# Decode attention with an MLP: group loads in a loop, wq and the last group inside TensorE's loop, heads transposed on VectorE, and a branch hint

## The chip, the core and the metric

The kernel runs on one core of a Trainium2 chip. A core has five engines, each with its own program: TensorE (PE, matmuls), VectorE (DVE), ScalarE (ACT), GpSimd (POOL) and SyncE (SP), which here only issues transfers. They meet in semaphores. Data moves from memory into the on-chip buffer by 16 DMA engines; matmuls write to PSUM. The metric is the device time of one execution in microseconds.

## The reference, cut to what matters

```python
xn = layernorm(x)                                    # x: 4 x 1 x 512
q  = (xn @ wq) as 4 x 32 heads x 128                 # wq: 512 x 4096
p  = softmax(q . k_cache * 128**-0.5)                # k_cache: 4 x 32 x 4096 x 128
o  = p . v_cache                                     # v_cache: the same shape
A   = o as 4 x 4096 @ wo                              # wo: 4096 x 512
B   = x1 + gelu(layernorm(x1) @ w3) @ w4              # w3: 512 x 1792, w4: 1792 x 512
out = x + A + B
```

x1 is xn: with one position the spatial shift leaves only zeros, so w1 and w2 have no effect and are not read. All is float32. K and V are 268 MB each; with wq, wo, w3 and w4 561 MB are read once.

## The kernel before

The 128 heads of the 4 batches are worked off in `NG` = 32 groups of 4 heads. One group's K, and one group's V, is a tile of 128 partitions x 16,384 columns (8.39 MB): partitions 32t to 32t+31 hold head t, each a stretch of 64 KB. Three such slots exist: K alternates between S1 (even groups) and S0 (odd groups), V lies in S2.

What is done for one group: VectorE spreads the query over the partitions (`qx`, `qb`, lines 324 and 327), multiplies K by it in place, in two halves (lines 330 and 332), sums over the 128 columns of each row (335, into `sc`), and finds the maximum (337 to 340). ScalarE takes the exponentials into `pw` (238). TensorE multiplies `pw` with V in 32 matmuls of 512 columns into `pv` (167); one small matmul sums the denominators (171); ScalarE copies `pv` (244); four small matmuls pick the heads out (176); and ScalarE keeps the result in `OS` (246). Then V's slot is free.

SP's program is written out, one instruction for each transfer. It issues V(g), waits until the sum over K(g) is done (`k_free`), issues K(g+2), waits until V(g) is used (`v_free`), and so on (lines 133 to 139). All its transfers stand in one queue in that order. At the start it issues wq in two halves into S2 and the first K in two halves; K(1) and V(0) wait for the query (`d_T`, line 131). The second half of the first K is passed on by POOL (lines 159, 160). At the end the last V goes to S1 as soon as K(30) is used up (141), w3 and w4 go to S2 when V(30) is used (143, 144), and wo goes to S0 in six pieces when K(31) is used (148).

TensorE's program is the query's matmuls (190), a loop over 31 groups, then, written out: three "spreads" of the heads of a batch over the partitions by a matmul (181), the last group's V, w3 (207), the last spread, and w4 (217). In a second block of code (from line 365) it multiplies wo piece by piece: rows 0 to 23 of each partition into `y`, in 512 columns, the others straight into `total`, in four quarters; ScalarE copies `y`, and four matmuls add that copy to `total` (381). Two copies and two transfers write the output.

Between the two blocks all engines meet.

Of the kernel before, what the change touches and what calls it, by code (L numbers as in the profile page):

```python
# [7 lines left out]
F32 = mybir.dt.float32  # L8
# [5 lines left out]
P = 128  # L14
# [6 lines left out]
def decode_block(ctx: ExitStack, tc: tile.TileContext, x, k, v, wq, wo, w3, w4, out):  # L21
# [26 lines left out]
    X = sbuf("X", [P, WC, B])  # L48
# [3 lines left out]
    mask = sbuf("mask", [P, 4])  # L52
# [7 lines left out]
    ot = sbuf("ot", [P, JB, HG])  # L60
    rec = sbuf("rec", [P, JB, HG])
    lt = sbuf("lt", [P, H, 4])

    pv, oz, total, y, pa, pb = (nc.alloc_psum_tensor(f"ps{i}", [P, 512], F32) for i in range(6))
# [7 lines left out]
    PIECES = ((0, 8), (8, 16), (16, 24), (24, 28), (28, 31), (31, 32))  # L72
    CUT = 24
    s_x, s_v, s_vl, s_kh, s_h = (sem(n) for n in ("sx", "sv", "svl", "skh", "sh"))
    s_wq = [sem(f"swq{n}") for n in range(2)]
    s_k = [sem(f"sk{n}") for n in range(2)]
    s_wo = s_k + [s_v, s_x, s_kh, s_h]
    d_self, g_a, c_done, d_T, k_free, v_free = (sem(n) for n in ("dself", "ga", "cd", "dT", "kf", "vf"))
# [6 lines left out]
    def group(flat, g):  # L85
        n = HG * S * DH
        return flat[g * n:(g + 1) * n].rearrange("(p r) -> p r", p=P)
# [4 lines left out]
    q_sb = S0[:, 4 * D:6 * D].rearrange("p (n f) -> p n f", n=2)  # L92
    qT = S0[:, 6 * D:8 * D]
    xp = S0[:, 8 * D:8 * D + 2 * P].rearrange("p (e c i) -> p e c i", e=2, c=NC)
    xnT = S0[:, 9 * D:9 * D + P].rearrange("p (c m) -> p c m", c=NC)
    wq_sb = S2[:, :].rearrange("p (c n) -> p c n", c=NC)
    w3_sb = S2[:, :NC * F].rearrange("p (c f) -> p c f", c=NC)
    w34 = NC * F + NF * D
    w4_sb = S2[:, NC * F:w34].rearrange("p (m n) -> p m n", m=NF)
    hs, gu, gt, gT = (S2[:, w34 + n * FT:w34 + (n + 1) * FT] for n in range(4))  # L100
    V3 = S2[:, :].rearrange("p (c d) -> p c d", c=C)
    VL = S1[:, :].rearrange("p (c d) -> p c d", c=C)
# [10 lines left out]

    with tc.tile_critical(no_gpsimd_drain=True), nc.Block(no_gpsimd_drain=True) as block:

        @block.sync
        def _(e):
            def load_k(g):
                e.dma_start(KS[g % 2][:, :], group(kf, g)).then_inc(s_k[g % 2], 16)

            def load_k_half(g, n, s):
                r = slice(n * ROW // 2, (n + 1) * ROW // 2)
                e.dma_start(KS[g % 2][:, r], group(kf, g)[:, r]).then_inc(s, 16)

            wq_r = wq.rearrange("(p c) n -> p c n", p=P)
            for n in range(2):
                c = slice(n * NC // 2, (n + 1) * NC // 2)
                e.dma_start(wq_sb[:, c, :], wq_r[:, c, :]).then_inc(s_wq[n], 16)
            load_k_half(0, 0, s_k[0])
            load_k_half(0, 1, s_kh)  # L130
            e.wait_ge(d_T, 2)
            load_k(1)
            for g in range(NG - 1):
                if g > 0:
                    take(e, v_free)
                e.dma_start(S2[:, :], group(vf, g)).then_inc(s_v, 16)
                if g + 2 < NG:
                    take(e, k_free)
                    load_k(g + 2)
            take(e, k_free)  # L140
            e.dma_start(S1[:, :], group(vf, NG - 1)).then_inc(s_vl, 16)
            take(e, v_free)
            e.dma_start(w3_sb, w3.rearrange("(p c) f -> p c f", p=P)).then_inc(s_wq[0], 16)
            e.dma_start(w4_sb, w4.rearrange("(p m) n -> p m n", p=P)).then_inc(s_wq[1], 16)
            take(e, k_free)
            wo_r = wo.rearrange("(p c) n -> p c n", p=P)
            for n, (c0, c1) in enumerate(PIECES):
                e.dma_start(wo_sb[:, c0:c1, :], wo_r[:, c0:c1, :]).then_inc(s_wo[n], 16)  # L148

        @block.gpsimd  # L150
        def _(e):
            e.memset(xs, 0.0).then_inc(g_a, 1)
            e.memset(ident[:, :], 0.0).then_inc(c_done, 1)
            e.memset(rs[:, :], 0.0)
            e.memset(pw[:, :, :], 0.0).then_inc(g_a, 1)
# [3 lines left out]
            take(e, s_kh, 16)  # L159
            e.wait_ge(c_done, 2).then_inc(s_h, NG)  # L160

        @block.tensor
        def _(e):
            def contract(V):
                for g in range(G4):
                    t = g % 4
                    i = mm(e, pv[32 * t:32 * t + 32, :], pw[:, g, :], V[:, 4 * g:4 * g + 4, :], g < 4, g >= G4 - 4)
                return i

            def outputs(done):  # L170
                i = mm(e, oz[:, HG:2 * HG], ones[:, :], rs[:, :], True, True)
                if done is not None:
                    i.then_inc(done, 1)
# [4 lines left out]

            def spread(b):
                take(e, d_p)  # L180
                mm(e, pa[:, 32 * b:32 * b + 32], lt[:, :, :], sel[:, :], True, True).then_inc(p_a, 1)

            e.wait_ge(d_T, 1)
            for c in range(NC):
                if c % (NC // 2) == 0:
                    take(e, s_wq[c // (NC // 2)], 16)
                w = wq_sb[:, c, :].rearrange("p (n j h d) -> p n h j d", n=2, j=JB // 2, h=HG)
                for n in range(2):
                    for h in range(HG):
                        i = mm(e, (pa, pb)[n][32 * h:32 * h + 32, :], xnT[:, c, :], w[:, n, h], c == 0, c == NC - 1)  # L190
                    if c == NC - 1:
                        i.then_inc(p_a, 1)

            with nc.Fori(0, NG - 1, 1, engines=[ET.PE]):
                take(e, s_v, 16)
                take(e, a_p)
                contract(V3).then_inc(p_a, 1)
                outputs(v_free)
            for b in range(B - 1):
                spread(b)  # L200
            take(e, a_p)
            take(e, s_vl, 16)
            contract(VL).then_inc(p_a, 1)
            e.wait_ge(s_wq[0], 16)
            for c in range(NC):
                for t in range(4):
                    i = mm(e, pb[32 * t:32 * t + 32, :FT], x1T[:, c, :], w3_sb[:, c, t * FT:(t + 1) * FT],
                           c == 0, c == NC - 1)
            i.then_inc(p_a, 1)
            outputs(None)  # L210
            spread(B - 1)
            mm(e, total[:, 0:P], ident[:, :], base[:, :], True, False)
            e.wait_ge(s_wq[1], 16)
            e.wait_ge(d_p, 1)
# [5 lines left out]
        def _(e):  # L220
# [5 lines left out]
            for n in range(2):  # L226
                take(e, p_a)
                e.mul(q_sb[:, n, :], (pa, pb)[n][:, :], DH ** -0.5).then_inc(a_d, 1)
            e.wait_ge(d_T, 2)
            e.activation(os[:, 0, 0:1], st[:, 3:4], AF.Exp)  # L230
            take(e, g_a)

            def weights():
# [6 lines left out]
                i.then_inc(a_p, 1)  # L240

            def outputs(o):
                take(e, p_a)
                e.copy(os[:, :, :], pv[:, :].rearrange("p (m d) -> p m d", m=4)).then_inc(a_p, 1)  # L244
# [3 lines left out]
            def spread(b):  # L248
                take(e, p_a)
                return e.copy(X[:, :, b], pa[:, 32 * b:32 * b + 32])  # L250

            with nc.Fori(0, NG - 1, 1, engines=[ET.Activation]) as g:
                weights()
                e.drain().then_inc(a_d, 1)
                outputs(OS[:, bass.ds(g, 1), :])
            weights()
            e.drain().then_inc(a_d, 1)
            for b in range(B - 1):
                spread(b).then_inc(c_done, 1)
            take(e, p_a)  # L260
            e.copy(os[:, :, :], pv[:, :].rearrange("p (m d) -> p m d", m=4)).then_inc(a_p, 1)
            take(e, p_a)
            e.copy(hs.rearrange("p (m i) -> p m i", i=32),
                   pb[:, :FT].rearrange("p (i m) -> p m i", i=32)).then_inc(a_d, 1)
            take(e, p_a)
            e.copy(OS[:, NG - 1:NG, :], oz[:, 0:2 * HG].unsqueeze(1)).then_inc(a_d, 1)
            e.wait_ge(d_a, 1)
            e.activation(gt, gu, AF.Tanh, scale=GELU_A).then_inc(a_d, 1)
            spread(B - 1)

        @block.vector
        def _(e):
            def own(i, n=1):
                i.then_inc(d_self, 1)
                take(e, d_self, n)
# [5 lines left out]
            own(e.reduce_sum(mask[:, :], ident[:, :].rearrange("p (q m) -> p q m", q=4), axis=AX.X))  # L281
# [142 lines left out]
```

## Time and profile before

| what | value |
|---|---|
| three runs | 1304.78, 1305.07, 1305.14 us; median 1305.07 |
| profiled execution, own time | 1304.94 us |
| its span, first to last instruction | 1303.2 us |
| read from memory | 561.00 MB, 430 GB/s over the span |
| mean granted TensorE clock | 0.627 |

Most rows of a profile give a line of the program, an engine, an operation, then the tile written and the tiles read. In a row of groups there follow the shapes, the count, the busy time in us and the mean of one in ns, and last the engine's idle time ahead of the group with what ended it. In a row in order of time the start and the length in us stand first. `SPq` is SP's queue: its rows are the moments at which a transfer is issued, not the transfer itself, and the profile gives the landing apart. `PEld` is TensorE's load of weights; a float32 matmul shows as two records and two loads.

### The profile page before, as it was taken

What the parts mean: (1) busy time and instruction counts of PE and PEld (TensorE: products, weight loads), DVE (VectorE), ACT (ScalarE), POOL (GpSimd) and SP (SyncE); (2) the same over time, 40 slices, a digit from 0 to 9 for tenths busy, and PEclk for the clock granted to TensorE, in tenths of its full rate; (3) what the DMA queues carried; (4) which work ended last, traced back from release to release, by engine and by line L of the source; (5) the groups of instructions that cost most, each with busy time, mean ns of one, the idle gap of its engine ahead of it and who ended that gap; (6) DMA issues with size and microseconds to landing.
All of it is one profiled execution on the core that took longest, in us unless ns stands there. A gap on an engine that the chain in (4) does not pass through costs nothing. (4 is left out here: it accounts for less than half of the span.)

```text
span 1303.2 us, 7027 instructions
## 1 busy us (share of the span) xinstructions
PE 364.8 (28%) x2622; PEld 130.6 (10%) x2622; DVE 1169.3 (90%) x343; ACT 98.9 (8%) x335; POOL 2.1 (0%) x9
## 2 busy tenths in 40 slices
PE   2032123333113333213333212333311333321347
PEld 0010001111001111001111000111000111100112
DVE  4999999999999999999999999999999999999971
ACT  1000000000000000000000000000000000000010
POOL 0000000000000000000000000000000000000000
PEclk9565566666566666566666556666556666655669
DMA  9999999999999999999999999999999999999998
GB/s 403 435 447 422 447 420 449 420 447 422 430 437 424 445 422 447 422 447 422 447 420 449 421 447 422 439 428 428 441 422 447 422 445 424 445 424 445 422 429 347
DMA packets 10830, 561.08 MB, mean 431 GB/s; under 512 B 1212, under 2 KB 1220, under 8 KB 1480
## 3 DMA queue, kind: packets, MB, share of 16 engines
q1 hardware_dynamic: 10808, 561.00, 99.6%
q8 instruction: 3, 0.05, 0.0%
q14 instruction: 3, 0.02, 0.0%
q10 hardware_dynamic: 16, 0.01, 0.0%
HBM read 561.00 MB, written 0.01 MB: 430 GB/s over the span
## 5 line engine op out<-in xcount | busy, mean ns | idle before, releaser
L335 DVE TENSOR_REDUCE sc<-slot 128x128 f32<-128x16384 f32 x32 | 551.0, 17220 | 8.2 <-DVEq L70 8.2
L112 PE MATMUL ps<-slot,pw 128*32 128x512 f32 x2048 | 294.9, 740 | 882.2 <-PEq L70 882.2
L330 DVE TENSOR_TENSOR slot<-slot,qb 128x8192 f32<-128x8192 f32 x32 | 278.1, 8692 | 43.6 <-DVEq L70 43.6
L332 DVE TENSOR_TENSOR slot<-slot,qb 128x8192 f32<-128x8192 f32 x32 | 277.9, 8684 | 2.1 <-DVEq L70 2.1
L112 PEld LDWEIGHTS ps<-slot,pw 128*32 128x32 f32 x2048 | 80.7, 133 | 1071.0 <-issue 1070.9
L238 ACT ACTIVATE pw<-sc,st 32x128 f32<-32x128 f32 x128 | 67.3, 525 | 243.0 <-ACTq L70 241.5
L244 ACT COPY os<-ps 128x512 f32<-128x512 f32 x31 | 18.1, 585 | 857.1 <-ACTq L70 857.1
L112 PE MATMUL ps<-sel,os 128*128 128x4 f32 x256 | 32.8, 252 | 17.5 <-PEq L70 17.5
L112 PEld LDWEIGHTS ps<-sel,os 128*128 128x128 f32 x256 | 31.0, 191 | 19.3 <-issue 19.3
L238 ACT ACTIVATION_READ_ACCUMULATOR pw<-sc,st 32x1 f32 x128 | 26.1, 204 | 0.0
L112 PE MATMUL ps<-slot 128*32 128x512 f32 x92 | 14.0, 747 | 18.8 <-PEq L70 17.6
L327 DVE STREAM_TRANSPOSE qb<-qx 128x128 f32<-128x128 f32 x32 | 10.0, 311 | 4.9 <-DVEq L70 0.5
L386 DVE COPY res<-ps 64x128 f32<-64x128 f32 x1 | 0.3, 283 | 15.2 <-PE ps L112 15.2
L337 DVE TENSOR_REDUCE st<-sc 128x1 f32<-128x128 f32 x32 | 9.2, 286 | 4.7
L356 DVE TENSOR_TENSOR slot<-slot 128x448 f32<-128x448 f32 x1 | 0.6, 624 | 13.1 <-DVEq L70 13.1
L112 PE MATMUL ps<-rs,ones 128*128 128x4 f32 x64 | 12.3, 263 | 0.0
L112 PEld LDWEIGHTS ps<-rs,ones 128*128 128x128 f32 x64 | 9.5, 188 | 26.7 <-issue 26.7
L324 DVE COPY qx<-Q 128x128 f32 x32 | 7.3, 227 | 4.9 <-issue 4.6
L339 DVE STREAM_TRANSPOSE mt<-mx 128x32 f32<-128x32 f32 x32 | 6.8, 211 | 4.7
L340 DVE TENSOR_REDUCE st<-mt 128x1 f32<-128x32 f32 x32 | 6.0, 186 | 4.8 <-DVEq L70 1.8
L338 DVE COPY mx<-st 128x32 f32<-128x32 f32 x32 | 5.8, 181 | 4.7
L246 ACT COPY OS<-ps 128x8 f32 x31 | 5.1, 165 | 42.4 <-ACTq L70 42.4
(58 smaller groups left out, 54.2 us busy)
## 6 DMA issues: line engine op xcount, KB each, us to landing
slot<-in_A_wq_dram SPq DMA_DIRECT2D x2, 4096.0 KB, 16.8
slot<-in_A_k_cache_dram SPq DMA_DIRECT2D x2, 4096.0 KB, 35.8
slot<-in_B_w_dram SPq DMA_DIRECT2D x2, 3584.0 KB, 22.7
slot<-in_A_wo_dram SPq DMA_DIRECT2D x3, 2048.0 KB, 30.1
slot<-in_A_wo_dram SPq DMA_DIRECT2D x1, 1024.0 KB
slot<-in_A_wo_dram SPq DMA_DIRECT2D x1, 768.0 KB, 37.9
slot<-in_A_v_cache_dram SPq DMA_DIRECT2D x32, 28.8
slot<-in_A_k_cache_dram SPq DMA_DIRECT2D x31, 42.3
```

The source lines that it names most:

```text
L112: return e.matmul(o, l, r, start=start, stop=stop)
L238: i = e.activation(o, sc[r, :].rearrange("p (g w) -> p g w", w=4), AF.Exp, bias=st[r, 1:2], scale=1.0, accum_out=rs[r, h:h + 1])
L244: e.copy(os[:, :, :], pv[:, :].rearrange("p (m d) -> p m d", m=4)).then_inc(a_p, 1)
L324: own(e.tensor_copy(qx[:, :].rearrange("p (h r) -> p h r", h=4), Q[:, bass.ds(g + n, 1), :].rearrange("p o h -> p (o h)").unsqueeze(2) .to ...
L327: own(e.transpose(qb[:, :], qx[:, :]))
L330: e.tensor_tensor(out=K[:, :C // 2, :], in0=K[:, :C // 2, :], in1=qw, op=ALU.mult).then_inc(d_self, 1)
L332: e.tensor_tensor(out=K[:, C // 2:, :], in0=K[:, C // 2:, :], in1=qw, op=ALU.mult).then_inc(d_self, 1)
L335: e.reduce_sum(sc[:, :], K, axis=AX.X).then_inc(d_self, 1)
L337: own(e.reduce_max(st[:, 0:1], sc[:, :], axis=AX.X), 2)
L338: own(e.tensor_copy(mx[:, :], st[:, 0:1].to_broadcast([P, 32])))
L339: own(e.transpose(mt[:, :], mx[:, :]))
L340: e.tensor_reduce(st[:, 1:2], mt[:, :], axis=AX.X, op=ALU.max, negate=True).then_inc(d_a, 1)
```

## The change

- A group is now made of four heads that lie four apart (`n t e` in the views `kf` and `vf`), so the source of each load of K and V is 4 x 32 rows of 64 KB, the four stretches of 32 rows 8.4 MB apart, where it was 128 rows in one stretch. The tile on the chip is the same.
- SP issues the groups' loads in a loop of 8 turns with 4 groups each; the addresses come from registers. The first K is one load. wq is loaded as 20/32 and 12/32 of each row; so is the last V.
- At the end w3 and w4 come first, into S1, and the last V comes behind them, into S2.
- TensorE's loop has 33 turns: the first multiplies wq by the input, which VectorE has written into columns 16 to 23 of `pw`; the last is the last group, with w3's matmuls ahead of it behind a branch. In each turn the last 12 of the 32 matmuls wait for `v_rest`, which POOL passes on for the first and the last turn and gives in advance for the others.
- ScalarE scales no query any more and runs its loop over all 32 groups; in the last turn it does its part of the MLP behind a branch.
- VectorE multiplies K in one instruction. The heads are turned by a transpose of 32 x 32 blocks (24 groups, and later the last 8) in place of the spreads. With that wo is read with its rows in another order, as 4 x 32 rows.
- wo's pieces end at rows 12, 20, 25, 28, 31 and 32 (before: 8, 16, 24, 28, 31 and 32), and rows 0 to 27 go into `y`.
- VectorE's program is aligned, and TensorE's program begins with a hint for the branch behind its last matmul, with padding behind that branch.

The core of the diff, with "..." where lines are left out:

```diff
+    X = sbuf("X", [P, B, H])
...
-    PIECES = ((0, 8), (8, 16), (16, 24), (24, 28), (28, 31), (31, 32))
-    CUT = 24
+    PIECES = ((0, 12), (12, 20), (20, 25), (25, 28), (28, 31), (31, 32))
+    CUT = 28
+    GF = 20
...
-    kf = k.rearrange("b h s d -> (b h s d)")
-    vf = v.rearrange("b h s d -> (b h s d)")
+    NB = B * 2
+    kf = k.rearrange("b (n t e) s d -> (b n) e t (s d)", n=2, t=HG).rearrange("m e t (p r) -> m e t p r", p=32)
+    vf = v.rearrange("b (n t e) s d -> (b n) e t (s d)", n=2, t=HG).rearrange("m e t (p r) -> m e t p r", p=32)
...
+    nc.vector.addr_align(128, offset=100, max_nops=0)
+    ahead = nc.tensor.mark_branch_hint_location()
...
+            e.dma_start(S2[:, FIRST], wq_r[:, FIRST]).then_inc(s_v, 16)
+            e.dma_start(S2[:, REST], wq_r[:, REST]).then_inc(s_q, 16)
+            load_k(0, 0)
+            e.wait_ge(d_T, 1)
+            load_k(0, 1)
+            with nc.Fori(0, NB, 1, engines=[ET.SP]) as m:
+                for i in range(3):
+                    load_v(m, i)
                     take(e, k_free)
+                    if i < 2:
+                        load_k(m, i + 2)
+                e.br_lt(m, NB - 1, on_true="sp_more", on_false="sp_next")
+                with nc.body("sp_more", valid_engines=[ET.SP]):
...
+                    load_k(after, 0)
+                    load_v(m, 3)
+                    take(e, k_free)
+                    load_k(after, 1)
+                    nc.br("sp_next", engines=[ET.SP])
+                nc.switch_bb("sp_next")
+            e.dma_start(w3_sb, w3.rearrange("(p c) f -> p c f", p=P)).then_inc(s_w3, 16)
+            e.dma_start(w4_sb, w4.rearrange("(p m) n -> p m n", p=P)).then_inc(s_w4, 16)
+            take(e, v_free)
+            last = src(vf, NB - 1, 3)
+            e.dma_start(S2[:, FIRST], last[:, :, FIRST]).then_inc(s_v, 16)
+            e.dma_start(S2[:, REST], last[:, :, REST]).then_inc(s_q, 16)
             take(e, k_free)
...
+            wo_r = wo.rearrange("(h q c) n -> q h (c n)", h=H, q=4)
...
+            with nc.Fori(0, NG + 1, 1, engines=pe) as g:
+                e.br_lt(g, NG, on_true="pe_turn", on_false="pe_mlp")
...
+                take(e, s_v, 16)
+                take(e, a_p)
+                for n in range(G4):
+                    if n == GF:
+                        take(e, v_rest)
+                    t = n % 4
+                    i = mm(e, pv[32 * t:32 * t + 32, :], pw[:, n, :], V[:, 4 * n:4 * n + 4, :], n < 4, n >= G4 - 4)
...
-                    e.tensor_tensor(out=K[:, :C // 2, :], in0=K[:, :C // 2, :], in1=qw, op=ALU.mult).then_inc(d_self, 1)
-                    take(e, s_h)
-                    e.tensor_tensor(out=K[:, C // 2:, :], in0=K[:, C // 2:, :], in1=qw, op=ALU.mult).then_inc(d_self, 1)
+                    own(e.tensor_tensor(out=K, in0=K, in1=qb[:, :].unsqueeze(1).to_broadcast([P, C, DH]), op=ALU.mult))
...
+                return e.transpose(X[:, b0:b1, :].rearrange("p b h -> p (b h)"), ot[:, b0:b1, :].rearrange("p b h -> p (b h)"))
...
         i.then_inc(g_a, 1)
+        e.br("pe_last").branch_hint(ahead)
+        with nc.body("pe_gap", valid_engines=[ET.PE]):
+            e.addr_align(256, offset=16, max_nops=0)
+            nc.br("pe_last", engines=[ET.PE])
+        nc.switch_bb("pe_last")
```

How the order of the program moves is seen best on the two engines on which the end rests. First SP's queue at its end, before (a row: line, operation, destination and source, shape of the tile):

```order
L119 DMA slot<-in_A_k_cache_dram 128x16384
L136 DMA slot<-in_A_v_cache_dram 128x16384
L141 DMA slot<-in_A_v_cache_dram 128x16384
L143 DMA slot<-in_B_w_dram 128x7168
L144 DMA slot<-in_B_w_dram 128x7168
L148 DMA slot<-in_A_wo_dram 128x4096 x3
L148 DMA slot<-in_A_wo_dram 128x2048
L148 DMA slot<-in_A_wo_dram 128x1536
L148 DMA slot<-in_A_wo_dram 128x512
```

And with the change, from the loop's end on:

```order
L130 REGISTER_ALU
L130 COMPARE_AND_BRANCH
L146 DMA slot<-in_B_w_dram 128x7168
L147 DMA slot<-in_B_w_dram 128x7168
L150 DMA slot<-in_A_v_cache_dram 128x1x10240
L151 DMA slot<-in_A_v_cache_dram 128x1x6144
L155 DMA slot<-in_A_wo_dram 128x1x6144
L155 DMA slot<-in_A_wo_dram 128x1x4096
L155 DMA slot<-in_A_wo_dram 128x1x2560
L155 DMA slot<-in_A_wo_dram 128x1x1536 x2
L155 DMA slot<-in_A_wo_dram 128x1x512
```

The last V has moved behind w3 and w4 and stands in two parts directly ahead of wo. Now TensorE from behind its loop to wo, before (`lt` is a batch's heads for a spread, `x1T` the MLP's input, `X` the heads for wo):

```order
L112 MATMUL ps<-sel,lt 128x32 x3
L112 MATMUL ps<-slot,pw 32x512 x32
L112 MATMUL ps<-slot,x1T 32x448 x16
L112 MATMUL ps<-rs,ones 128x4
L112 MATMUL ps<-sel,os 128x4 x4
L112 MATMUL ps<-sel,lt 128x32
L112 MATMUL ps<-base,ident 128x128
L112 MATMUL ps<-slot 32x512 x14
L114 UNCONDITIONAL_BRANCH x2
L419 UNCONDITIONAL_BRANCH
L112 MATMUL ps<-slot,X 4x512 x24
```

And with the change, from the MLP's code in the loop (run in the last turn alone) to wo:

```order
L105 MATMUL ps<-slot,x1T 32x448 x16
L183 UNCONDITIONAL_BRANCH
L105 MATMUL ps<-slot,pw 32x512 x32
L105 MATMUL ps<-rs,ones 128x4
L105 MATMUL ps<-sel,os 128x4 x4
L174 REGISTER_ALU
L174 COMPARE_AND_BRANCH
L105 MATMUL ps<-base,ident 128x128
L105 MATMUL ps<-slot 32x512 x14
L109 UNCONDITIONAL_BRANCH x2
L414 UNCONDITIONAL_BRANCH
L105 MATMUL ps<-slot,X 4x512 x28
```

The spreads are gone, w3's matmuls have moved ahead of the last V's, and 28 matmuls of 512 columns with wo stand where 24 stood.

More of the change, by code (lines that the diff above doesn't have):

```diff
@@ L59, in decode_block @@
     res = sbuf("res", [2 * 32, 2, P])
[L60 to L64, printed above, removed]
+    ot = sbuf("ot", [P, B, H])
+    rec = sbuf("rec", [P, NG, HG])
+    warm = sbuf("warm", [P, 1])
+    pv, oz, total, y, pb = (nc.alloc_psum_tensor(f"ps{i}", [P, 512], F32) for i in range(5))
     def sem(name):
@@ L117, in _ @@
         def _(e):
[L118 to L128, printed above, removed]
@@ L142, in _, with src, load_k @@
[L142 to L146, printed above, removed]
+            def src(flat, m, i):
+                return flat[m, i] if isinstance(m, int) else flat[bass.ds(m, 1), i].rearrange("m t p r -> (m t) p r")
+            def load_k(m, i):
+                e.dma_start(KS[i % 2][:, :], src(kf, m, i)).then_inc(s_k[i % 2], 16)
@@ L154, in _ @@
             e.memset(rs[:, :], 0.0)
-            e.memset(pw[:, :, :], 0.0).then_inc(g_a, 1)
+            e.memset(pw[:, :, :], 0.0)
             e.wait_ge(c_done, 1)
@@ L177, in outputs @@
                 i.then_inc(p_a, 1)
[L179 to L211, printed above, removed]
             mm(e, total[:, 0:P], ident[:, :], base[:, :], True, False)
-            e.wait_ge(s_wq[1], 16)
-            e.wait_ge(d_p, 1)
+            e.wait_ge(s_w4, 16)
+            take(e, d_p)
             for m in range(NF):
@@ L225, in _, with values @@
                 e.activation(st[:, 2:3], st[:, 1:2], AF.Sqrt, bias=st[:, 3:4], scale=1.0 / D).then_inc(a_d, 1)
-            for n in range(2):
+            def values():
                 take(e, p_a)
[L228 to L231, printed above, removed]
+                return e.copy(os[:, :, :], pv[:, :].rearrange("p (m d) -> p m d", m=4)).then_inc(a_p, 1)
+            values()
+            e.drain().then_inc(a_d, 1)
+            take(e, p_a)
+            e.activation(warm[:, :], st[:, 3:4], AF.Exp)
             def weights():
@@ L240, in weights @@
                 i.then_inc(a_p, 1)
+                e.drain().then_inc(a_d, 1)
             def outputs(o):
-                take(e, p_a)
-                e.copy(os[:, :, :], pv[:, :].rearrange("p (m d) -> p m d", m=4)).then_inc(a_p, 1)
+                values()
                 take(e, p_a)
                 return e.copy(o, oz[:, 0:2 * HG].unsqueeze(1))
[L248 to L252, printed above, removed]
+            act = [ET.Activation]
@@ L253, in _ @@
+            with nc.Fori(0, NG, 1, engines=act) as g:
                 weights()
-                e.drain().then_inc(a_d, 1)
+                e.br_lt(g, NG - 1, on_true="act_values", on_false="act_mlp")
+                with nc.body("act_mlp", valid_engines=act):
+                    take(e, p_a)
+                    e.copy(hs.rearrange("p (m i) -> p m i", i=32),
+                           pb[:, :FT].rearrange("p (i m) -> p m i", i=32)).then_inc(a_d, 1)
+                    take(e, d_a)
+                    e.activation(gt, gu, AF.Tanh, scale=GELU_A).then_inc(a_d, 1)
+                    nc.br("act_values", engines=act)
+                nc.switch_bb("act_values")
@@ L255, in _ @@
                 outputs(OS[:, bass.ds(g, 1), :])
-            weights()
             e.drain().then_inc(a_d, 1)
[L258 to L269, printed above, removed]
         @block.vector
         def _(e):
-            def own(i, n=1):
+            done = [0]
+            def mark(i):
                 i.then_inc(d_self, 1)
-                take(e, d_self, n)
+                done[0] += 1
+            def own(i):
+                mark(i)
+                e.wait_ge(d_self, done[0])
@@ L277, in _, with clear, rows @@
+            def clear():
+                take(e, d_self, done[0])
+                done[0] = 0
+            def rows(t):
+                return slice(32 * t, 32 * t + 32)
             e.memset(ones[:, :], 1.0)
@@ L358, in _ @@
             e.tensor_mul(gu, gu, hs).then_inc(d_a, 1)
-            normalised(B - 1)
-            e.wait_ge(a_d, 1)
+            take(e, a_d)
             own(e.tensor_scalar(gt, gt, 1.0, 0.5, op0=ALU.add, op1=ALU.mult))
```

153 lines of the change are left out of this document (72 added, 81 removed).

## The prediction

> **What bounds the kernel now.** I read the page first, then the stretches of time, then the queue's issues in order of time, then the chain that ended last. From the page: the engines' busy time and two DMA queues (packets, MB, share of 16 engines' span).
>
> ```profile
> PE 364.8 (28%) x2622; PEld 130.6 (10%) x2622; DVE 1169.3 (90%) x343; ACT 98.9 (8%) x335; POOL 2.1 (0%) x9
> ...
> q1 hardware_dynamic: 10808, 561.00, 99.6%
> ...
> q10 hardware_dynamic: 16, 0.01, 0.0%
> ```
>
> VectorE looks like the bound at 90%, but SP's queue is at 99.6%. The stretches decide it (start:end, length, then each engine's busy time, the granted clock, the DMA share and GB/s):
>
> ```profile
> 0.00:3.00 3.00, 0.00 (x0) 0.00 (x0) 0.29 (x3) 0.00 (x0) 2.09 (x9) 1.00 0.60 175
> ...
> 100.00:400.00 300.00, 83.07 (x570) 29.20 (x574) 286.40 (x73) 22.16 (x78) 0.00 (x0) 0.60 1.00 433
> 400.00:700.00 300.00, 76.66 (x544) 28.01 (x536) 277.52 (x73) 22.86 (x80) 0.00 (x0) 0.61 1.00 433
> 700.00:1000.00 300.00, 85.01 (x592) 30.45 (x592) 277.78 (x71) 22.86 (x80) 0.00 (x0) 0.62 1.00 433
> ...
> 1290.00:1295.00 5.00, 3.94 (x40) 0.90 (x44) 0.00 (x0) 0.00 (x0) 0.00 (x0) 1.00 0.96 403
> 1295.00:1299.00 4.00, 2.81 (x60) 1.27 (x56) 0.00 (x0) 0.58 (x1) 0.00 (x0) 1.00 0.69 275
> ```
>
> Three stretches of 300 us give 433 GB/s at a DMA share of 1.00, although VectorE's work in them differs by 9 us. So the transfers set the pace. VectorE's groups and the landings say the same:
>
> ```profile
> L335 DVE TENSOR_REDUCE sc<-slot 128x128 f32<-128x16384 f32 x32 | 551.0, 17220 | 8.2 <-DVEq L70 8.2
> L330 DVE TENSOR_TENSOR slot<-slot,qb 128x8192 f32<-128x8192 f32 x32 | 278.1, 8692 | 43.6 <-DVEq L70 43.6
> L332 DVE TENSOR_TENSOR slot<-slot,qb 128x8192 f32<-128x8192 f32 x32 | 277.9, 8684 | 2.1 <-DVEq L70 2.1
> ```
> ```profile
> slot<-in_A_v_cache_dram SPq DMA_DIRECT2D x32, 28.8
> slot<-in_A_k_cache_dram SPq DMA_DIRECT2D x31, 42.3
> ```
>
> VectorE waits 43.6/32 = 1.4 us per group for K. A load of 8.39 MB takes 8.39/433 = 19.4 us by itself but lands 28.8 us after its issue (V) and 42.3 us (K): when a load is issued, 9.4 us and 22.9 us of earlier work still stand in the queue. That is the cover which the issuing side has. The queue's own issues (start, length, line):
>
> ```profile
> 29.18 0.33 SPq L119 DMA_DIRECT2D slot<-in_A_k_cache_dram  x1
> 29.55 0.43 SPq L136 DMA_DIRECT2D slot<-in_A_v_cache_dram  x1
> 69.84 0.33 SPq L119 DMA_DIRECT2D slot<-in_A_k_cache_dram  x1
> 91.67 0.33 SPq L136 DMA_DIRECT2D slot<-in_A_v_cache_dram  x1
> ...
> 407.68 0.33 SPq L119 DMA_DIRECT2D slot<-in_A_k_cache_dram  x1
> ...
> 1181.72 0.33 SPq L119 DMA_DIRECT2D slot<-in_A_k_cache_dram  x1
> 1214.54 0.33 SPq L136 DMA_DIRECT2D slot<-in_A_v_cache_dram  x1
> 1220.42 0.33 SPq L141 DMA_DIRECT2D slot<-in_A_v_cache_dram  x1
> 1252.67 0.33 SPq L143 DMA_DIRECT2D slot<-in_B_w_dram  x1
> ...
> 1259.13 2.70 SPq L148 DMA_DIRECT2D slot<-in_A_wo_dram  x6
> ```
>
> Twenty periods lie between 407.68 and 1181.72: 38.70 us each, and 16.78 MB per period is again 433 GB/s. The chain that ended last is the stream's end and little else:
>
> ```profile
> 1260.93 37.92 DMA slot<-in_A_wo_dram
> ...
> 1298.89 1.10 PE ps L112 x32
> ...
> 1300.02 0.28 DVE res L386
> ```
>
> So 561.0 MB at 433 GB/s is 1295.6 us; with about 1.8 us before the first byte (3 us x 175 is 0.53 MB, or 1.2 us of the stream) that ends near 1297.4; the stream ends at 1298.85, and 1303.2 - 1298.85 = 4.35 us follow. The execution's own time is 1304.94, 1.74 over its span; the median of the three runs is 1305.07, 0.13 above it. I sum against 1304.94.
>
> **The change part by part.** *Bytes:* the same 561.0 MB; wq, the last V and wo are only cut differently. At 433 GB/s: 0.
>
> *The loop's arithmetic.* Two multiplications (8.69 + 8.68) become one over 16,384 columns, about 17.4 us, and a semaphore step goes: under 0.2 us per group from an engine that already waits 1.4. Nothing at the end: 0. SP's loop adds register work before each issue; an issue takes 0.33 us, and if it tripled, 9.4 us of queue cover V and 22.9 cover K: 0. TensorE's jump over the MLP's code in each turn stands before the wait for V: 0; should it cost 1 us after V has landed, the 9.4 still hide it.
>
> *The start.* K's first load is no longer halved, so VectorE begins its first group later. The rows (V's landings: least, median, most):
>
> ```profile
> 43.51 8.69 DVE L332 TENSOR_TENSOR slot<-slot,qb 128x8192 f32<-128x8192 f32 x1 [2.13 <-DVEq L70]
> ```
> ```profile
> DMA to landing us min/median/max: 28.1/28.8/52.4
> ```
>
> The second half of K came at about 43.4. Now the whole multiplication starts there and ends at 60.8, and the reduction at about 78.3, against 69.84 now: VectorE is 8.5 us later. K2 is issued on that, and the queue then still holds V0, which landed at 29.55 + 52.4 = 81.95: 3.6 us are left, so the queue does not run dry. The next two: V1 waits for TensorE's turn after V0's landing, as now (91.67); K3 comes at about 78.3 + 37.3 = 115.6, five us before V1's landing at 81.95 + 2 x 19.4 = 120.7. VectorE then needs 38.70 - 1.4 = 37.3 us a group when it need not wait, and wins 1.4 back in each. Cost 0; if the queue should run dry at K2, up to 2 us (an issue's start-up, from the 1.8 us before the first byte, beyond what the 3.6 covers). K1 waits for Q: one transpose of 512 columns and one copy instead of 1024 columns and two scalings against two small copies and a memset ahead of the matmuls; within 1 us of 29.18, while K0 lands at 43.4: 14 us of cover, 0.
>
> *The tail* is where cover is thin. w3 and w4 now come before the last V. Issue times stay (1220.42, 1252.67, 1259.13), and at 1252.67 the queue still holds about half of w3 and w4 (7.34 MB, 17 us, behind V30, which had landed when TensorE began on it at 1243.71), so it is not empty. The last V now ends where wo begins, 19.4 us before 1298.85: at 1279.5, its first 20/32 at 1272.2. TensorE's new wait, for the rest of wq or of this V by way of POOL, holds back its last 12 matmuls and the sums behind them; POOL releases the turns between ahead of time. ScalarE's last turn now waits for the MLP's matmuls and VectorE's GELU before it copies sums: w3 lands near 1252, so this is over near 1266, long before 1283. From 1272.2 TensorE has a row of work. Its rows at two paces (two matmuls are four loads), the steps after a group's matmuls, and the present tail:
>
> ```profile
> 1285.79 0.23 PEld L112 LDWEIGHTS ps<-slot 128*32 128x32 f32 x4 [0.63 <-issue]
> 1286.64 0.22 PEld L112 LDWEIGHTS ps<-slot 128*32 128x32 f32 x4 [0.63 <-issue]
> ...
> 1292.34 0.11 PEld L112 LDWEIGHTS ps<-slot,X 128*4 128x4 f32 x4 [0.32 <-issue]
> 1292.77 0.11 PEld L112 LDWEIGHTS ps<-slot,X 128*4 128x4 f32 x4 [0.32 <-issue]
> ```
> ```profile
> 1214.06 0.39 PE L112 MATMUL ps<-rs,ones 128*128 128x4 f32 x2
> ...
> 1216.24 0.17 ACT L246 COPY OS<-ps 128x8 f32 x1 [1.37 <-ACTq L70]
> ...
> 1243.71 8.55 PE L112 MATMUL ps<-slot,pw 128*32 128x512 f32 x64 [27.67 <-PEq L70]
> ...
> 1284.96 4.96 PE L112 MATMUL ps<-slot 128*32 128x512 f32 x28 [1.19 <-DVE slot L363]
> ...
> 1291.06 5.37 PE L112 MATMUL ps<-slot,X 128*4 128x512 f32 x48 [1.13 <-SPq L365]
> ...
> 1296.50 0.58 ACT L384 COPY os<-ps 128x512 f32<-128x512 f32 x1 [12.69 <-PE ps L112]
> ```
>
> A 512-column matmul takes 0.43 us after an idle stretch and 0.21 once running. The last 12 matmuls of V end at 1279.5 + 2.6 to 5.1, middle 1283.3; the sums and copies behind them take 1214.06 to 1216.41, 2.35 us: 1285.7. The 14 matmuls with w4 (4.96 us with a cold start, 3.0 without) run beside VectorE's normalisation and end at about 1290; the hand-over between the blocks took 1.13: wo starts at 1291.1, as it does now (1291.06). The 28 rows of wo that go into y need 28 x 0.21 = 6.0 us, to 1297.1, and they wait for pieces anyway. What is new is that y takes four more rows: its copy (0.58) moves behind piece 25 to 28, to about 1298.5, just ahead of the last pieces. The end stays at 1300.0. Bounds: if V's part and w4 run cold throughout, wo starts at 1294.6 and the end moves to about 1302.1, **+2.1**. On the other side the stream's last 9 us lose (5 x 30 + 4 x 158)/433 = 1.8 us against full rate; other piece sizes could win that back, **-1.8**. I take -0.1. VectorE's four spreads of the outputs by matmul go; their work lay beside the stream: 0.
>
> *The branch hint and the padding.* The hint is one instruction at the start of TensorE's program. What it may hide, a fetch of code behind the last matmul, would lie beside the output's transfer (from 1300.02 + 0.28 to the span's end): 0; with that cover gone, the nearest row is the hand-over's 1.13.
>
> Sum: 1304.94 + 0 + 0 - 0.1 = **1304.8**.
>
> **Rivals.** *Four engines instead of sixteen (slower).* This is one mechanism in one place: the sources of K, V and wo become 4 x 32 rows where they were 128. Queue q1 carries 75 transfers of 128 rows and half the output (4 rows): 75 x 128 + 4 = 9604 rows. Of its 10808 packets 1204 are left, which is 75 x 16 + 4. Queue q10 carries x and the other half, 4 rows each: 8 rows of 16 packets, 8 left. So, if each engine used closes a transfer with one packet, a transfer of 128 rows runs on 16 engines and one of four rows on four. If the outer count of four decides, 64 K and V loads and wo, 545 MB, go at 433/4 = 108 GB/s: 5,040 us, with the other 16 MB about **5,080 us**. It decides as soon as the outer count, not the number of rows, shares out the work. The trace can't tell the two apart: where it shows four, there were only four rows, and every load changed here keeps 128 rows of the same length, whose nearest rows show 16. I take those: chance 0.1.
> [...] No run here shows a pattern of 4 x 32 rows.
>
> *Rows far apart in memory (slower).* The four heads of a load lie 8.4 MB apart. A loss of 1% of the rate costs 13 us: 1318. Against it: within a head the rows stay together, and the 433 doesn't move between stretches. Chance 0.04.
> [...]
>
> *TensorE late in the tail:* the cold bound, +2.1, with a dry queue at the start up to +4: 1307 to 1309. Chance 0.12, of which a third is beyond 0.2%.
>
> *The stream's ends win:* -1.8 at the end and up to a microsecond at the start: 1302. Chance 0.22, over half of it beyond 0.2%, since the rate too may rise a little with the new order.
>
> **How the numbers follow.** Forecast (the stream as it is, 1303 to 1306) 0.52, rivals as above. A measurement of this kernel can tell about 0.2%, 2.6 us, from no change. Slower: 0.1 + 0.04 + 0.04 = 0.18; faster 0.13; same 0.69. The range 1300.8 to 1308.5 takes in both tails and leaves out four engines, the row pitch and a little of the ends, under 0.2 together.
>
> **What would show it.** Right: 433 GB/s and a share of 1.00 in the three middle stretches, K issues 38.7 us apart, VectorE's first reduction ending near 78 with no dip in GB/s there, wo's first matmul near 1291. Wrong: about 108 GB/s with a DMA share near a quarter, and fewer closing packets on q1 (four engines); a lower rate at a full share (row pitch); wo's matmuls still running behind the last landing (TensorE late).

## The result: 5507 us, and the profile after

| kernel | median, range of runs (us) | ratio to before, 95% interval |
|---|---|---|
| before | 1304.96 (1304.78 to 1305.35) | |
| after | 5506.83 (5460.88 to 7238.61) | 4.21 [4.19, 4.23] |

The change makes the kernel 4.2 times slower; the forecast was 1304.8. The top of the range is one run of six that stands apart; the interval is without it. The profiled execution took 5537.42 us. From the page of after: the span, the engines, the DMA share and GB/s in 40 slices of 138 us, and the queues (packets, MB, share of 16 engines).

```profile
span 5535.6 us, 6990 instructions
...
PE 369.4 (7%) x2600; PEld 130.1 (2%) x2600; DVE 1165.5 (21%) x307; ACT 97.4 (2%) x330; POOL 2.1 (0%) x9
...
DMA  3222222222222222222222222222222222222421
GB/s 108 59 63 67 77 88 101 103 90 95 101 108 110 108 108 109 109 108 108 110 108 108 109 109 108 108 110 108 108 108 109 108 108 109 108 108 108 134 70 76
...
q1 hardware_dynamic: 9956, 560.99, 25.5%
```

The bytes are the same, and VectorE works 1165.5 us as before (1169.3). What changed is the DMA share, 25.5% where it was 99.6%: no compute engine is slower, the transfers are. The queue's packets tell on how many engines they ran. Of 9956 packets 9604 are rows, as before; 352 close transfers. Four transfers of 16 (wq twice, w3, w4) are 64; 288 are left for 71 loads of K, V and wo and half the output: four each, and a share of a quarter is four of 16 engines. In the stretches (start:end, length, busy time of the five engines, clock, DMA share, GB/s) a second thing shows:

```profile
50.00:100.00 50.00, 0.00 (x0) 0.00 (x0) 0.00 (x0) 0.00 (x0) 0.00 (x0) 0.50 0.25 55
100.00:400.00 300.00, 0.00 (x0) 0.00 (x0) 71.64 (x16) 2.11 (x8) 0.00 (x0) 0.50 0.25 61
400.00:700.00 300.00, 10.68 (x74) 3.82 (x74) 35.79 (x8) 2.86 (x10) 0.00 (x0) 0.51 0.25 71
700.00:1000.00 300.00, 20.98 (x148) 7.53 (x148) 53.53 (x10) 5.71 (x20) 0.00 (x0) 0.53 0.25 97
1000.00:1300.00 300.00, 21.43 (x148) 7.66 (x148) 53.96 (x15) 5.72 (x20) 0.00 (x0) 0.53 0.25 94
1300.00:1600.00 300.00, 20.81 (x148) 7.48 (x148) 71.64 (x16) 5.72 (x20) 0.00 (x0) 0.53 0.25 102
2000.00:3000.00 1000.00, 74.97 (x518) 26.81 (x518) 214.92 (x48) 20.00 (x70) 0.00 (x0) 0.53 0.25 109
3000.00:4000.00 1000.00, 62.56 (x444) 22.55 (x444) 240.92 (x50) 17.15 (x60) 0.00 (x0) 0.53 0.25 109
...
5300.00:5400.00 100.00, 13.06 (x106) 4.59 (x106) 4.55 (x9) 4.02 (x12) 0.00 (x0) 0.57 0.23 74
5400.00:5500.00 100.00, 15.60 (x104) 5.09 (x104) 0.78 (x3) 0.75 (x2) 0.00 (x0) 0.59 0.22 83
5500.00:5536.00 36.00, 12.58 (x96) 2.83 (x96) 0.28 (x1) 0.85 (x2) 0.00 (x0) 0.59 0.15 56
```

From 50 to 4000 us the share is a quarter, but the rate is not: 61 GB/s at first, 109 later. 109 is a quarter of the 433 before; at 61 four engines are busy all the time and move little more than half of what they can. VectorE's group of multiplications, and the issues of K and V in SP's queue, show what this does to the rest:

```profile
L324 DVE TENSOR_TENSOR slot<-slot,qb 128x16384 f32<-128x16384 f32 x32 | 551.2, 17225 | 4071.4 <-DVEq L69 4071.4
```
```profile
2051.33 0.53 SPq L121 DMA_DIRECT2D slot<-in_A_v_cache_dram  x1
2052.25 0.55 SPq L117 DMA_DIRECT2D slot<-in_A_k_cache_dram  x1
2205.45 0.53 SPq L121 DMA_DIRECT2D slot<-in_A_v_cache_dram  x1
2206.25 0.55 SPq L117 DMA_DIRECT2D slot<-in_A_k_cache_dram  x1
```

VectorE waits 4071.4 us for K where it waited 45.7 (43.6 + 2.1), and a group takes 154 us in place of 38.7: 16.78 MB / 154 us is 109 GB/s.

### The profile page after: what moved, and what is told of

It reads as the page before. It is cut to its first block, busy times and chain, and to the rows that moved or that the text cites. A ratio compares the mean times of both kernels' runs of the same rounds, so it can differ in the third digit from the quotient of the medians.

```text
span 5535.6 us, 6990 instructions
## 1 busy us (share of the span) xinstructions
PE 369.4 (7%) x2600; PEld 130.1 (2%) x2600; DVE 1165.5 (21%) x307; ACT 97.4 (2%) x330; POOL 2.1 (0%) x9
## 3 DMA queue, kind: packets, MB, share of 16 engines
q1 hardware_dynamic: 9956, 560.99, 25.5%
## 5 line engine op out<-in xcount | busy, mean ns | idle before, releaser
L324 DVE TENSOR_TENSOR slot<-slot,qb 128x16384 f32<-128x16384 f32 x32 | 551.2, 17225 | 4071.4 <-DVEq L69 4071.4
L105 PE MATMUL ps<-slot,X 128*4 128x512 f32 (+1 forms) x88 | 12.2, 668 | 59.7 <-SPq L355 51.9
```

The lines of the kernel that those rows point to most:

```text
L105: return e.matmul(o, l, r, start=start, stop=stop)
L324: own(e.tensor_tensor(out=K, in0=K, in1=qb[:, :].unsqueeze(1).to_broadcast([P, C, DH]), op=ALU.mult))
```

## The experiments

Two questions: does the outer count of the source (the size of its outermost dimension, here 4) pick the number of engines, or the distance between the four stretches make them slow; and does any other part of the change cost anything? The theory is the rival with four engines; it is set against the row pitch, and against a cost in the loop, the order or the hint.

**The change with whole quarters (e1).** Each load of K, V, wq and wo becomes four transfers of 32 rows; for K and V each is one head.

```diff
+            def load(o, parts, s):
+                for t in range(4):
+                    e.dma_start(o[32 * t:32 * t + 32, :], parts[t]).then_inc(s, 16)
...
-                e.dma_start(KS[i % 2][:, :], src(kf, m, i)).then_inc(s_k[i % 2], 16)
+                load(KS[i % 2][:, :], src(kf, m, i), s_k[i % 2])
```

> The changed kernel with each load of K, V, wq and wo issued as four transfers of 32 rows (one head, or one quarter of wo, each), all else as changed. Engine count: 32 rows can be shared by 16 engines, so the rate returns to about 433 GB/s and the time to 1303 to 1325 (wo and K then write 32 partitions at a time, which could cost some of the rate). Row distance: the four heads still lie 8.4 MB apart, so it stays above 2,000 us. Loop and register addresses: stays near 5,500 us.

Measured: 2693.67 us, ratio 2.063 [2.059, 2.067]. Two stretches of it:

```profile
100.00:400.00 300.00, 29.88 (x222) 11.04 (x222) 158.96 (x34) 10.68 (x38) 0.00 (x0) 0.55 1.00 206
...
1000.00:1300.00 300.00, 31.89 (x226) 11.36 (x229) 143.28 (x32) 8.57 (x30) 0.00 (x0) 0.55 1.00 206
```

All 16 engines are busy again (share 1.00), so the outer count of 4 left twelve of them idle. But 206 GB/s is under half of 433, and the expected 1303 to 1325 us was missed: a second limit holds that doesn't show in the share. By its time alone this run would fit the row distance too.

**The kernel before with other outer counts (e2, e3, e4).** Only the source of K and V is changed: `cnt` stretches of 128/`cnt` rows, 8.4 MB apart. (Queries, keys and values no longer belong together.)

```diff
-        return flat[g * n:(g + 1) * n].rearrange("(p r) -> p r", p=P)
+        cnt, pad = 4, 0
+        start = (g // cnt) * cnt * n + (g % cnt) * (n // cnt)
...
+        return apart[:, 0:n // cnt].rearrange("t (p r) -> t p r", p=P // cnt)
```

> The kernel before with one edit: each load of K and V takes its 128 rows from four stretches of 32 rows, 8.4 MB apart (heads and queries no longer match). No loop, no register addresses. Engine count: four engines, DMA share 0.25, K and V at 108 GB/s, 5,000 to 5,500 us. Loop and register addresses: 1305 us. Row distance: also slow, but at a share of 1.00.

> As the run with 4 x 32 rows, but eight stretches of 16 rows, 8.4 MB apart. Engine count: eight engines, share 0.5, 217 GB/s, about 2,500 us. Row distance: as slow as 4 x 32 rows or slower, since twice as many far streams are read at a time.

> As before, sixteen stretches of 8 rows, 8.4 MB apart. Engine count: sixteen engines, share 1.00, about 1305 us if distance costs nothing. [...]

Measured: 5285.23, 4558.49 and 2646.02 us (one run each). The rate in slices with 4 stretches, and a stretch of time each with 8 and with 16:

```profile
GB/s 116 66 68 76 86 101 107 109 109 107 109 109 107 109 109 107 109 109 107 109 109 107 109 109 108 109 109 108 109 109 108 109 109 108 109 109 108 108 121 143
...
q1 hardware_dynamic: 10028, 560.99, 26.3%
```
```profile
100.00:400.00 300.00, 10.05 (x74) 3.65 (x74) 99.05 (x26) 4.96 (x18) 0.00 (x0) 0.52 0.50 107
```
```profile
100.00:400.00 300.00, 41.34 (x296) 14.93 (x296) 143.58 (x36) 11.20 (x39) 0.00 (x0) 0.56 1.01 209
```

The kernel before with this one edit is as slow as the changed one. The share goes with the outer count: 0.25, 0.50, 1.00. So do the closing packets: 10028 - 9604 = 424 are 65 loads x 4, ten transfers x 16 and 4 for the output. The rate does not, and the times expected for 8 x 16 (2,500 us) and 16 x 8 (1305 us) were missed: eight engines start at the 107 GB/s which four reach later, and sixteen get 209. By its time, twice that of before, 16 x 8 leaves room for a cost of the distance.

**Distance or pattern.** Three runs tell these apart: quarters of 32 rows with memory in one stretch (e5, the transfers of the first experiment in the kernel before); 128 rows that lie 2.1 MB apart (e6); 4 x 32 rows with a single row of 64 KB left out between the stretches (e7). The edits of e6 and of e7:

```diff
-        return flat[g * n:(g + 1) * n].rearrange("(p r) -> p r", p=P)
+        return flat.rearrange("(p g r) -> g p r", p=P, g=NG)[g]
```
```diff
+        start = min(g * n, flat.shape[0] - n - 4 * ROW)
+        apart = flat[start:start + n + 4 * ROW].rearrange("(t x) -> t x", t=4)
+        return apart[:, 0:n // 4].rearrange("t (p r) -> t p r", p=32)
```

> The kernel before with one edit: each load of K and V is issued as four transfers of 32 rows, all 128 rows still in one stretch of memory (no far rows, sixteen engines). Shared way into the buffer (sixteen engines that write 32 neighbouring partitions at a time): 206 GB/s at a share of 1.00, about 2,600 us. Row distance: 433 GB/s, 1305 us.

> The kernel before with one edit: each load of K and V is 128 rows, as before, but with 2.1 MB between one row and the next (the rows of a group come from 128 heads; scores and values no longer belong together). Shared way into the buffer, or engine count: nothing changes, 433 GB/s, 1305 us. Row distance: near half rate at a share of 1.00, 2,000 us or more.

> The kernel before with one edit: each load of K and V as 4 x 32 rows whose four stretches lie 2.16 MB apart, one row skipped between them (some rows of the caches are read twice and some not). Engine count with a shared way: as the run with 4 x 32 far rows, share 0.25, about 60 GB/s at first and 108 later, 5,100 to 5,500 us. Row distance: faster than that, to 1305 us.

Measured: 2650.09, 1330.22 and 5297.02 us (one run each). A stretch of e5, one of e6, and the slices of e7:

```profile
100.00:400.00 300.00, 41.71 (x296) 15.13 (x296) 143.57 (x36) 9.94 (x35) 0.00 (x0) 0.56 1.00 206
```
```profile
400.00:700.00 300.00, 84.93 (x592) 30.47 (x592) 274.85 (x71) 22.65 (x79) 0.00 (x0) 0.62 1.00 428
```
```profile
GB/s 116 66 68 74 88 101 108 109 109 109 107 109 109 109 108 108 109 109 109 107 108 109 109 109 107 109 109 109 109 107 109 109 109 109 107 109 109 109 119 133
```

Every row 2.1 MB from the next costs 25 us of 1305; a gap of one row in the 4 x 32 pattern costs as much as 8.4 MB; and e5, with no gap at all, is as slow as e1. Distance is not it, the pattern is.

**Why busy engines are slow.** The rates at first were 55 to 67 GB/s with four engines (after, e2, e7), 107 with eight (e3), and 206 to 209 with sixteen (e4, e5). Per engine that is 14 to 17, 13 and 13 GB/s, 48 to 62% of the 433/16 = 27.1 in the kernel before. The time of a row says the same. In the trace's records of single packets, which the views here sum up and don't list, a row of 64 KB took 2.42 us in the kernel before (median), which is 27.1 GB/s; in after the median was 4.8 us between 100 and 400 us and 2.42 us from 2000 us on. In 16 x 8 rows (e4) and in the quarters (e5) the share and the rate between 100 and 400 us make it 5.1 us on average. So an engine that is counted as busy can take about twice as long for a row.

The distance in memory does not tell the slow patterns from the fast ones. The author supposed that it is the place written on the chip: that engines which start together and walk through their rows in step crowd on the same way into the buffer (the expectations speak of a shared way, and of ports). No run shows such a way, so the test can only move the place.

The test (e12) keeps four engines and moves what they write: quarters of 32 partitions, each from 4 stretches of 8 rows. If each engine takes one stretch, which no record here shows, the four begin at partitions 0, 8, 16 and 24 of a quarter, where in e7 they begin at 0, 32, 64 and 96. Without a slow start, 536.9 MB at the 108.5 GB/s of e7's later stretches and 24.1 MB at 433 are 4,948 + 56 = 5,004 us; with one, about the 5297 of e7.

```diff
+        start = min(g * n, flat.shape[0] - n - 16 * ROW)
+        apart = flat[start:start + n + 16 * ROW].rearrange("(t j x) -> t j x", t=4, j=4)
+        return apart[:, :, 0:n // 16].rearrange("t j (p r) -> t j p r", p=8)
...
+                    e.dma_start(o[32 * t:32 * t + 32, :], i[t]).then_inc(s, 16)
```

> The kernel before; each load of K and V is four transfers, one for each quarter of the partitions (32), and the source of each transfer is 4 stretches of 8 rows of 64 KB, with one row left out between the stretches (so some keys and values are other rows than the reference's, and the output is not the reference's). [...]

Measured: 5053.69 us (one run), in slices:

```profile
DMA  3222222222222222222222222222222222222235
GB/s 156 109 109 108 108 109 108 108 109 108 108 108 109 108 108 108 109 108 108 108 109 108 108 109 108 108 108 109 108 108 108 109 108 108 108 109 108 108 126 147
```

108 to 109 GB/s from the second slice to the 38th, at the same share of 0.25, which makes 2.4 us for a row on average: the slow start is gone. The run also has shorter transfers and shorter stretches than e7, so it doesn't move the place alone; but a cause on the memory's side would have to be the same for stretches 2.2 MB (e7) and 8.4 MB apart (e2), and for none (e5, with sixteen engines). That the place written sets the pace stays the author's estimate.

How 4 x 32 rows get out of the slow start (e7 gets 67 GB/s between 100 and 400 us, 84 in the next 300 us and 107 between 700 and 1000) shows in the packets that close a transfer, four for each. In the trace of after these come as two pairs. The two of a pair are 2.4 and 1.5 us apart at 176 to 191 us, 5.7 and 5.1 at 551 to 601, and 9.5 both at 922 to 993 us; from 1525 to 5144 us all are 9.5 apart, and from 2000 to 5000 us the rate is 108 to 109 GB/s. That is close to four rows of 2.42 us: if each packet is one engine's, the engines of a pair drift apart by about four rows. In e4 the rate stays at 206 to 214 GB/s from the second slice to the last but one; why it doesn't rise there is open.

**The rest of the change (e8).** Groups of neighbouring heads again, so that K and V are 128 rows; wo stays in the order that VectorE's transpose demands, as quarters of 32 rows.

```diff
-    kf = k.rearrange("b (n t e) s d -> (b n) e t (s d)", n=2, t=HG).rearrange("m e t (p r) -> m e t p r", p=32)
+    kf = k.rearrange("b (n e t) s d -> (b n) e (t s d)", n=2, t=HG).rearrange("m e (p r) -> m e p r", p=P)
...
-                e.dma_start(wo_sb[:, c0:c1, :], wo_r[:, :, c0 * D:c1 * D]).then_inc(s_wo[n], 16)
+                for q in range(4):
+                    e.dma_start(S0[32 * q:32 * q + 32, c0 * D:c1 * D], wo_r[q, :, c0 * D:c1 * D]).then_inc(s_wo[n], 16)
```

> The changed kernel with groups of four neighbouring heads: each load of K and V is 128 rows in one stretch again; TensorE and ScalarE take the columns in another order to suit. wo comes as four transfers of 32 rows for each piece. All else of the change stays (loop, register addresses, order at the end, branch hint). If the pattern of the loads is all that is wrong with the change: 433 GB/s until wo, which comes at 206 GB/s and so takes 41 us where it took 19: 1305 + 21 = about 1326 us. If loop or register addresses cost anything: more than that.

Measured: 1324.47 us, ratio 1.0145 [1.0128, 1.0162]. In the middle, and while wo runs:

```profile
400.00:700.00 300.00, 78.91 (x548) 28.66 (x540) 277.10 (x64) 25.39 (x80) 0.00 (x0) 0.60 1.00 434
...
1280.00:1290.00 10.00, 5.58 (x34) 2.38 (x34) 0.00 (x0) 0.58 (x1) 0.00 (x0) 0.83 0.95 199
1290.00:1300.00 10.00, 5.80 (x43) 1.56 (x46) 0.76 (x3) 0.17 (x1) 0.00 (x0) 0.89 0.97 208
```

434 GB/s with the loop of loads and all else; only wo, 8.39 MB at 199 to 213 where it had 433, is late: 8.39/204 - 8.39/433 = 22 us, against 19.4 measured.

Two kernels then are to give wo its rate back, in two ways. In e9 wo is read as before the change, in 128 rows, and a matmul of 128 columns brings the heads into that order. In e10 ScalarE issues the quarters of partitions 64 to 127 on its own queue. A third, e11, is e9 without the hint.

```diff
+            mm(e, pb[:, 0:P], perm[:, :], X[:, :, :].rearrange("p b h -> p (b h)"),
+               True, True).then_inc(p_a, 1)
...
+            e.copy(Xp[:, :, :].rearrange("p b h -> p (b h)"), pb[:, 0:P])
...
+            wo_r = wo.rearrange("(p c) n -> p (c n)", p=P)
...
+                e.dma_start(S0[:, c0 * D:c1 * D], wo_r[:, c0 * D:c1 * D]).then_inc(s_wo[n], 16)
```
```diff
-                for q in range(4):
+                for q in range(2):
...
+                        for q in (2, 3):
+                            e.dma_start(S0[32 * q:32 * q + 32, c0 * D:c1 * D], wo_r[q, :, c0 * D:c1 * D]).then_inc(s_wo[n], 16)
```

> The kernel of neighbouring heads again, but wo is read as before the change (128 rows, row p from 32 consecutive rows of wo), and one more matmul of TensorE (128 columns, by a permutation matrix) with a copy by ScalarE brings the normalised outputs into that order. All else of the change stays: the loop of loads, the order at the end, the transposes, the hint. If the outer count of 4 and the ports it writes to are the whole of the loss: wo goes at about 430 GB/s, lands near 1299, its first matmul near 1292, and the time is 1303 to 1308 (before: 1305; 1 to 2 us of it may be the extra matmul and copy). If something else of the change also costs, as the remainder of e8 leaves room for: over 1310, with wo's landing late in spite of 430 GB/s or TensorE still at work behind the last landing.

> The kernel of neighbouring heads again (wo in quarters of 32 rows), but ScalarE issues the quarters of partitions 64 to 127 on its own queue, in its last turn of the loop, and SP those of partitions 0 to 63. [...] If the number of transfers or their length alone makes wo slow: no gain, 1322 to 1327.

> The kernel of e9 without the early branch hint and the padding behind the last matmul. The prediction put the hint at 0: within 0.5 us of e9. If the hint hides a fetch of code at the end: 1 to 2 us slower than e9, with TensorE or ScalarE idle for that long in front of the last copies.

Measured: e9 1305.85 us, ratio 1.0007 [0.9998, 1.0016]; e10 1332.19, 1.0204 [1.0188, 1.0220]; e11 1306.09, 1.0009 [1.0000, 1.0018]. Two stretches of e9 and its last landing and what follows, in the chain that ended last:

```profile
400.00:700.00 300.00, 76.42 (x552) 27.94 (x543) 277.00 (x64) 25.38 (x80) 0.00 (x0) 0.62 1.00 433
...
1290.00:1295.00 5.00, 4.09 (x40) 0.98 (x40) 0.00 (x0) 0.00 (x0) 0.00 (x0) 1.00 1.00 417
```
```profile
1261.08 38.16 DMA slot<-in_A_wo_dram
...
1299.28 1.32 PE ps L107 x40
```

With 128 rows everywhere the 4,202 us are gone. The interval of e9 takes in no change, but ten of its eleven runs lie above all 21 of before: of its 0.9 us some may be real, and the added matmul and copy are in it. e11 lies 0.24 us from e9, inside both intervals: the hint is worth nothing that these runs can tell.

The two queues were meant to give a gain, and e10 is slower than e8, not faster. The rate while wo was under way:

```profile
1270.00:1280.00 10.00, 0.00 (x0) 0.00 (x0) 3.31 (x6) 0.84 (x2) 0.00 (x0) 0.50 0.99 202
1280.00:1290.00 10.00, 2.03 (x12) 0.69 (x16) 0.00 (x0) 0.00 (x0) 0.00 (x0) 0.50 0.92 191
1290.00:1300.00 10.00, 4.58 (x32) 1.03 (x24) 0.00 (x0) 0.00 (x0) 0.00 (x0) 0.84 1.01 228
1300.00:1310.00 10.00, 1.36 (x8) 0.46 (x12) 0.00 (x0) 0.00 (x0) 0.00 (x0) 0.50 0.99 235
1310.00:1320.00 10.00, 8.66 (x60) 3.08 (x52) 0.76 (x3) 0.75 (x2) 0.00 (x0) 0.86 0.99 260
```

Two queues to the two halves did not add up: 191 to 260 GB/s, 223 on average, where 128 rows get 433. The quarters on ScalarE's queue ran beside the last V, which is 128 rows: TensorE began on it at 1287.97 in place of 1273.64 in e8. In which order an engine serves two queues was not tried. The 223 GB/s, against 199 to 213 in e8, have V among them, so this run is no clean test of the two queues.

No version beat the kernel before; e9 comes within 1 us of it, and nothing in its profile points further, since its stream runs at the same rate and its last landing is 0.4 us later.

## Why the prediction was wrong

**The step that failed** is the term for the bytes, the first of the change: "the same 561.0 MB; wq, the last V and wo are only cut differently. At 433 GB/s: 0." It rested on "every load changed here keeps 128 rows of the same length, whose nearest rows show 16. I take those". The rival "Four engines instead of sixteen", at a chance of 0.1, was what happened: e2 alone, one edit of the source in the kernel before, gives 5285 us, and e9, without that pattern, 1306. The trace before did bear on it: its closing packets were 16 for an outer count of 128 and 4 for one of 4. By the number of rows on the chip 128 looked nearest; by the outer count the rows of four were nearest, and they said four. The trace left open which of the two decides; the runs with 128 rows in each load show the outer count, with shares of 0.25, 0.50 and 1.00 for 4, 8 and 16 (e2, e3, e4). With nothing in the trace against four engines, a chance of 0.1 was too low.

**The rival's price**, 5,080 us, holds for four engines at 108 to 109 GB/s (e12: 5054, with wo still on all sixteen; wo at 108 GB/s would add 58). The profiled execution of after took 457 more. At 108.5 GB/s the stretches from 50 to 100 us (55 GB/s) and from 100 to 1600 us (61, 71, 97, 94 and 102 GB/s) would have needed 25 and 325 us less, and the last 236 us, with the last V and wo at 74, 83 and 56 GB/s, 73 us less: 423 of the 457. Four engines were named; that they can run at 55 to 61 GB/s at first was not in it.

**Loop arithmetic, 0:** right as far as it can be told apart. e8 and e9 run at 433 to 434 GB/s with SP's loop, the single multiplication and TensorE's branch.

**The start, 0:** right. In e9, VectorE's first reduction, two issues of SP, and the stretch around them:

```profile
60.37 17.22 DVE L334 TENSOR_REDUCE sc<-slot 128x128 f32<-128x16384 f32 x1
```
```profile
77.88 0.34 SPq L119 DMA_DIRECT2D slot<-in_A_k_cache_dram  x1
...
114.22 0.33 SPq L119 DMA_DIRECT2D slot<-in_A_k_cache_dram  x1
```
```profile
65.00:85.00 20.00, 3.16 (x16) 0.90 (x20) 19.58 (x8) 2.42 (x8) 0.00 (x0) 0.50 0.99 426
```

It ends at 77.6 (78.3 predicted), K3 goes out at 114.2 (115.6), and the stream has no hole.

**The tail, -0.1:** right in its steps, as e9 shows, where the permutation stands in addition; the whole of e9 came out 0.9 us above before. TensorE's end in e9:

```profile
1280.47 2.78 PE L107 MATMUL ps<-slot,pw 128*32 128x512 f32 x24 [0.20 <-PEq L71]
...
1285.41 3.63 PE L107 MATMUL ps<-slot 128*32 128x512 f32 x28
1288.96 0.49 PE L107 MATMUL ps<-X,perm 128*128 128x128 f32 x2
1290.91 4.48 PE L107 MATMUL ps<-slot,Xp 128*4 128x512 f32 x40 [1.46 <-SPq L361]
```

The last V's matmuls end at 1283.25 (1283.3 predicted), those with w4 at 1289.0 (about 1290), and wo starts at 1290.9 (1291.1). The last matmul ends at 1300.6, not 1300.0, as the last piece lands 0.4 us later than before. (The cold bound, redone from its own rows, puts wo at 1294.1 and not 1294.6; nothing hangs on it.) The hint's 0 stands by e11.

**The other rivals:** rows far apart in memory were not what made the change slow: e7, with one row left out, is as slow as e2 with 8.4 MB. 128 rows of 64 KB that lie 2.1 MB apart (e6) still get 427 to 429 GB/s in the middle stretches. TensorE late and the stream's ends came to 1 us in e9, inside its interval.

## What to carry to other kernels

For each load, look at the outermost dimension of the source as the program writes it, not only at the tile on the chip: reading four blocks in one instruction left four of sixteen engines at work, and cost more than any compute edit could give. A busy share of 1.00 is not yet the full rate (206 GB/s against 433): check GB/s beside it, and keep 128 rows outermost in one transfer, as in the loads that got 433 here; where another order of rows is wanted, one small matmul on the data already on the chip cost at most about a microsecond here.

## What the runs showed of the hardware that was not expected

- Engines that are busy all the time can move half: 61 GB/s at a share of 0.25 in after, and 109 at the same share later. A row of 64 KB took 4.8 us there between 100 and 400 us, and 2.42 from 2000 us on (medians). With 8 x 16 rows (e3) the rate rises from 107 GB/s in the second slice to 152 in the 38th, at 4,300 us, without any change in the program's loads.
- 16 x 8 rows, although on all 16 engines, get 209 GB/s, nearly the same as quarters of 32 rows (206).
- An issue of SP, 0.3 to 0.6 us for most transfers, took up to 75.20 us for wo's pieces in after; in the chain that ended last:

```profile
5317.40 75.20 SPq L155
...
5392.64 47.40 SPq L155
...
5440.66 57.51 SPq L155
```

They stand behind transfers that run on four engines; why the issue itself blocks was not tried.
